# A written plan for the preparation of rows in a feed-forward stage, six relu buffers, and two folds moved ahead

## The chip, the cores and the metric

The kernel runs on one core of one Trainium2 chip. A core has five engines that run side by side, each through its own list of instructions in order: TensorE (PE in the profile, with PEld for its weight loads) multiplies matrices into PSUM, VectorE (DVE) and ScalarE (ACT) work elementwise and read PSUM and SBUF, GpSimd (POOL) works elementwise on SBUF, and SyncE (SP) issues transfers. An engine that reaches an instruction whose input isn't there stops, and everything behind it in its list stops too. The metric is the device time of one execution in microseconds (us), the median of several runs; a profiled execution gives a trace of every instruction.

## The reference

Only what is computed matters here:

```
def reference(A_x, A_w_r, A_w_i, B_x, B_w1, B_b1, B_w2, B_b2):
    x = A_x                                             # 1 x 2048 x 512, bf16
    X = rfft2(layernorm(x)) * (A_w_r + 1j * A_w_i)      # 2048 x 257 weights
    h = x + irfft2(X).bf16()
    r = relu(layernorm(h) @ B_w1 + B_b1)                # 512 -> 1792
    return h + (r * r) @ B_w2 + B_b2                    # 1792 -> 512
```

A spectral filter over both axes with a residual, then a feed-forward part with squared relu and another residual. Layer norms have no learned scale; each is over the 512 columns of a row.

## The kernel before

Everything is one core's work and stays in SBUF. The 2048 rows are kept as 16 groups of 128 rows. The Fourier transforms are matmuls against tables of sines and cosines that the kernel makes itself.

*First stage (lines 204 to 330).* For each group a row's mean and variance are found, by `bn_stats` and `bn_aggr` on VectorE (`ln1_stats`) or by two passes with accumulation on ScalarE (`ln1_sums`). `ln1_rstd` makes (variance + epsilon) to the power -0.5 with two GpSimd instructions. `ln1_fold` multiplies a table KF by it, one VectorE instruction for each group, into KFr, and `stage1` uses KFr as the moving operand of two groups' matmuls. The rows of x come in five loads: groups 0-1, 2-3, 4-7, 8-11, 12-15. Around the change the order is: statistics of groups 0 and 1, scale of 0 and 1, statistics of groups 2 and 4 (interleaved: both `bn_stats`, then both `bn_aggr`), folds of 0 and 1, `stage1(0)`.

*Middle (lines 340 to 530)*: three more transform stages and the product with the spectral weights in eight pairs of frequencies, ending in the tile T2 for all groups at once. The change doesn't touch it.

*Feed-forward part (lines 540 to 815).* The groups are taken in five chunks: CHUNKS = (0,1), (2-4), (5-8), (9-12), (13-15). A chunk of n groups is a moving operand of 128n columns. `mlp_slots(c)` makes its list of slots: 14 `up` slots, each four matmuls of W1 against UT into one PSUM bank `ph` (three of them), then a relu on ScalarE into a buffer `rl`, then the square on VectorE into `act`; then for each group three `down` slots of 5, 5 and 4 matmuls against W2 into a bank `po` (two of them), after which VectorE adds `hb` (that is h + b2, made on GpSimd, line 729, told to wait for the squares of f = 1, 4, 7, 10 of the chunk) and the result is stored. The last group of all is done in two halves (`last`).

While chunk c runs, chunk c + 1 is prepared. Its steps for a group g are:

- `s5`: four TensorE matmuls into a bank `pp` (three banks serve `pp`), the last transform along the columns, then two ScalarE copies out of it into V and H.
- `s5b`: four VectorE instructions that combine even and odd parts of V and H into R.
- `s6`: one TensorE matmul of R into a `pp` bank, the last transform along the rows.
- `s6a`: VectorE adds x and gives h (tile `hs`), which frees the bank.
- `s6b`: the statistics of h, on ScalarE for every second group of a chunk from 2 on (two passes, `on_act`), else on VectorE.

After all groups: `rstd` (square root on ScalarE, reciprocal on VectorE), `norm` (one VectorE instruction for each group, into u), and `transp` twice: TensorE transposes, one half of the columns each, with one ScalarE copy and one VectorE copy into UT, the operand of the next chunk's `up` slots.

What sets the order is a planner. `run(c)` walks through the slots, adds up their modelled TensorE costs (0.22 for each group of an `up` slot and so on), and after each slot puts out the preparation pieces that are due. `prep_steps` gives each piece a due time, by formula: evenly spaced rounds of s6(g-2), s5(g), s5b(g-1), s6a and s6b(g-2), from about 2n + 7.5 before the chunk's end to 7.3 before it, then `rstd`, `norm`, and the two `transp` at 2.4 and 1.7 before the end. `pin` then fixes this order on every engine, so the program's order is each engine's order.

Of the kernel before, what the change touches and what calls it, by code (L numbers as in the profile page):

```python
# [9 lines left out]
ALU = mybir.AluOpType  # L10
ACT = mybir.ActivationFunctionType
FP32 = mybir.dt.float32
BF16 = mybir.dt.bfloat16
I32 = mybir.dt.int32
I16 = mybir.dt.int16
P = 128
# [18 lines left out]
def kernel(  # L35
# [16 lines left out]
    nc = tc.nc  # L52
# [7 lines left out]
    EPS = 1e-5  # L60
# [41 lines left out]
    def after(ins, first, why):  # L102
        tc.add_manual_dep(ins.ins, first.ins.name,
                          mybir.DependencyInfo(mybir.DependencyClass.Sync, mybir.DependencyReason.DATA), reason=why)
        return ins
# [105 lines left out]
    def ln1_stats(*mine):  # L211
        sts = {}
        for k in range(len(mine) + 1):
            if k < len(mine):
                g = mine[k]
                sts[g] = st = fwd.tile([P, 6], FP32, tag="st", bufs=4, name="st")
                nc.vector.bn_stats(st[:], xs[:, g, :])  # L217
            if k > 0:
                g = mine[k - 1]
                nc.vector.bn_aggr(mv1[:, g, :], sts.pop(g)[:])  # L220

    def ln1_rstd(a, b):
        nc.gpsimd.tensor_scalar(rs1[:, a:b], mv1[:, a:b, 1], EPS, None, ALU.add)
        nc.gpsimd.tensor_tensor(rs1[:, a:b], rs1[:, a:b], mhalf[:, 0:b - a], ALU.pow)

    def ln1_fold(a, b, eng=nc.vector):
        for g in range(a, b):
            last = eng.tensor_scalar(KFr[:, g, :], KF[:], rs1[:, g:g + 1], None, ALU.mult)  # L228
        return last
# [32 lines left out]
    def angles_c(sl):  # L262
        return nc.gpsimd.tensor_scalar(fiE[1][:].rearrange("p (a b) -> p a b", a=9)[:, sl],
                                       fiE[0][:].rearrange("p (a b) -> p a b", a=9)[:, sl], 1.0, float(QT), ALU.mult,
                                       ALU.add)
# [8 lines left out]
    after(nc.gpsimd.tensor_scalar(fiG[:, 0:256], idxL[:, 0:256], cols[:, 0:1], float(QT), ALU.mult, ALU.add), fk,  # L274
          "the angles of the first stage first")
    nc.gpsimd.tensor_scalar(fiG[:, 256:512], idxL[:, 256:512], cols[:, 0:1], float(HT), ALU.mult, ALU.add)
    ln1_rstd(0, 2)
    ln1_stats(2, 4)
    f01 = ln1_fold(0, 2)
    after(angles_c(slice(0, 9)), f01, "not beside the folds")  # L280
    stage1(0, 12)
    ln1_sums(13)
# [273 lines left out]
    def s5(g, ahead=False):  # L556

        pe = bank("p5", "po", 2) if ahead else bank("p5", "pp", 3)  # L560
        for lt, tb, o in ((1, GI[:, 1, 0:129], 0), (3, GI[:, 3, 1:128], 129), (0, GI[:, 0, 0:128], 256),
                          (2, GIa[:, 1024:1152], 384)):
            nc.tensor.matmul(pe[:, o:o + tb.shape[1]], lhsT=T2[:, 2 * (lt % 2) + lt // 2, g].rearrange("p q s -> p (q s)"), rhs=tb,  # L563
                             start=True, stop=True)

        def rest():
            V = ffn.tile([P, 2, 2, 128], BF16, tag="V", bufs=3, name="V")
            H = ffn.tile([P, 2, 256], BF16, tag="H", bufs=3, name="H")
            nc.scalar.copy(V[:].rearrange("p e h c -> p (e h c)"), pe[:])  # L569
            nc.scalar.copy(H[:, :, 0:129:128], pe[:].rearrange("p (e h c) -> p e h c", e=2, h=2)[:, :, :, 0])  # L570
            Rs[g] = V, H

        if ahead:
            return rest
        rest()
# [38 lines left out]
    def s6(g):  # L614
        py = bank("p6", "pp", 3)
        if g == 0:
            nc.tensor.matmul(py[:], lhsT=identW[:], rhs=xs[:, 0, :], start=True, stop=False)
            nc.tensor.matmul(py[:], lhsT=KI[:], rhs=Rs.pop(g)[:], start=False, stop=True)
            nc.scalar.activation(hs[:, 0, :], py[:], ACT.Copy, scale=WSC, accum_out=mv2[:, 0, 0:1])
            return  # L620
        nc.tensor.matmul(py[:], lhsT=KI[:], rhs=Rs.pop(g)[:], start=True, stop=True)  # L621
        Ys[g] = py

    def s6a(g):
        nc.vector.scalar_tensor_tensor(hs[:, g, :], Ys.pop(g)[:], WSC, xs[:, g, :], ALU.mult, ALU.add)  # L625
# [16 lines left out]
    def on_act(c, g):  # L642

        return g == 0 if c < 2 else (g - CHUNKS[c][0]) % 2 == 0
# [23 lines left out]
    def transp(c, half):  # L668
# [13 lines left out]
        else:  # L682
            nc.vector.tensor_copy(dst, src)

    def prep_steps(c, total):

        a, b = CHUNKS[c]
        n = b - a
        first = 2 if c == 1 else 0
        end = total - 7.3  # L690
        t0 = 1.2 if c == 1 else total - 0.5 - 2.0 * n - 7.0
        gap = (end - t0) / (n + 1 - first)
        t0 = end - (n + 1) * gap
        steps = [(0.4, 0, rest[1])] if c == 1 else []
        for k in range(first, n + 2):
            t = t0 + k * gap
            if k >= 2:
                steps.append((t, 0.22, lambda g=a + k - 2: s6(g)))
            if k < n:
                steps.append((t, 0.22, lambda g=a + k: s5(g)))  # L700
            if 1 <= k <= n:
                steps.append((t + 0.1, 0, lambda g=a + k - 1: s5b(g)))
            if k >= 2:
                steps.append((t + 0.1, 0, lambda g=a + k - 2: (s6a(g), s6b(g, on_act(c, g)))))
        t = t0 + (n + 1) * gap
        steps.append((t + 1.6, 0, lambda: rstd(c)))
        steps.append((t + 2.2, 0, lambda: norm(c)))
        steps.append((total - 2.4, 0.12 * n, lambda: transp(c, 0)))
        steps.append((total - 1.7, 0.12 * n, lambda: transp(c, 1)))
        return steps  # L710

    def mlp_slots(c):
        a, b = CHUNKS[c]
        n = P * (b - a)
        UT = UTs[c]
        act = ffn.tile([P, NF, 512], BF16, tag="act", bufs=2, name="act")
        slots = []

        def up(f):
            ph = bank("ph", "ph", 3)  # L720
            for d in range(ND):
                nc.tensor.matmul(ph[:, 0:n], lhsT=W1[:, d, bass.ts(f, P)], rhs=UT[:, d, 0:n],  # L722
                                 start=(d == 0), stop=(d == ND - 1))
            rl = ffn.tile([P, 512], BF16, tag="rl", bufs=3, name="rl")
            nc.scalar.activation(rl[:, 0:n], ph[:, 0:n], ACT.Relu, bias=b1f[:, f:f + 1], scale=1.0)  # L725
            sq = nc.vector.tensor_tensor(act[:, f, 0:n], rl[:, 0:n], rl[:, 0:n], ALU.mult)  # L726
            mine = [a + f // 3] if c and f % 3 == 1 and f // 3 < b - a else range(a, b) if not c and f == NF - 1 else []
            for g in mine:
                add = nc.gpsimd.tensor_tensor(hb[:, g, :], hs[:, g, :], b2b[:], ALU.add)  # L729
                tc.add_manual_dep(add.ins, sq.ins.name,  # L730
                                  mybir.DependencyInfo(mybir.DependencyClass.Sync, mybir.DependencyReason.DATA),
                                  reason="not before this square")

        state = {}

        def last(i):
            g = a + i
            ot = ffn.tile([P, D], BF16, tag="ot", bufs=3, name="ot")
            for h in range(2):
                po = bank("po", "po", 2)  # L740
                sl = slice(256 * h, 256 * h + 256)
                for f in range(NF):
                    nc.tensor.matmul(po[:, 0:256], lhsT=act[:, f, bass.ts(i, P)], rhs=W2[:, f, sl], start=(f == 0),  # L743
                                     stop=(f == NF - 1))
                nc.vector.tensor_tensor(ot[:, sl], po[:, 0:256], hb[:, g, sl], ALU.add)
                nc.sync.dma_start(ov[:, g, sl], ot[:, sl])

        def down(i, f0, f1):
            if c == 4 and i == b - a - 1:
                return last(i) if f0 == 0 else None  # L750
            if f0 == 0:
                state[i] = bank("po", "po", 2)
            po = state[i]
            for f in range(f0, f1):
                nc.tensor.matmul(po[:], lhsT=act[:, f, bass.ts(i, P)], rhs=W2[:, f, :], start=(f == 0), stop=(f == NF - 1))  # L755
            if f1 == NF:
                g = a + i
                ot = ffn.tile([P, D], BF16, tag="ot", bufs=3, name="ot")
                nc.vector.tensor_tensor(ot[:], po[:], hb[:, g, :], ALU.add)  # L759
                nc.sync.dma_start(ov[:, g, :], ot[:])  # L760

        for f in range(NF):
            slots.append((0.22 * (b - a), lambda f=f: up(f)))
        for i in range(b - a):
            for f0, f1 in ((0, 5), (5, 10), (10, NF)):
                slots.append((0.22 * (f1 - f0), lambda i=i, f0=f0, f1=f1: down(i, f0, f1)))
        return slots
# [76 lines left out]
```

## Time and profile before

The time is 172.0 us, the median of three runs (171.52 to 172.26). The profiled execution's span is 171.0 us, at full TensorE clock.

| engine | busy us | share |
|---|---|---|
| TensorE | 154.7 | 90% |
| VectorE | 127.6 | 75% |
| ScalarE | 108.7 | 64% |
| GpSimd | 37.2 | 22% |

The first 20 us load and normalize; from 20 to 54 the transforms run; the first `up` matmul of chunk 0 starts at 54.39, those of chunks 1 to 4 at 70.50, 94.40, 122.40 and 149.38; the last matmul ends at 167.7 and the last store lands at the end of the span. A busy share says how long an engine had something in it, and is an average over stages with different limits. A wait, by contrast, names the engine that was waited for. In lists of waits the columns are the total us, the number of waits and the longest. In timelines they are start, length, engine, line, operation, output and input, and in brackets the idle time before it and what ended that. Runs of the same line are merged ("x6").

### The profile page before, as it was taken

How to read it: one execution, taken by the hardware profiler on the slowest of the kernel's cores; microseconds unless marked ns; L12 is line 12 of the kernel's file. 1: busy time of each engine (PE TensorE's matmuls, PEld its weight loads, DVE VectorE, ACT ScalarE, POOL GpSimd, SP SyncE). 2: the span in 40 equal slices, each digit the busy share in tenths (PEclk: the TensorE clock that was granted, in tenths of full speed). 3: DMA queues.
4: the chain of work that ended last, by engine and by line, in shares of the span. 5: the costliest groups of instructions: out<-in, count | busy, mean ns of one | idle time of the engine just before them, and what ended most of it. 6: DMA issues, size and time to landing. Idle time of an engine off the chain costs nothing.

```text
span 171.0 us, 2777 instructions
## 1 busy us (share of the span) xinstructions
PE 154.7 (90%) x976; PEld 89.0 (52%) x976; DVE 127.6 (75%) x319; ACT 108.7 (64%) x201; POOL 37.2 (22%) x65
## 2 busy tenths in 40 slices
PE   3679999899898889998699999999999999999992
PEld 1257667677754663565235444544544454456461
DVE  7799899999847888589597577698767587578320
ACT  4799887999956652498624677554377634478200
POOL 7588850000000005052000135000025200025000
PEclk9999999999999999999999999999999999999999
DMA  5997299996000000100000100000100000010011
GB/s 125 345 287 89 76 190 201 395 359 86 0 0 4 0 0 2 58 9 0 0 0 31 61 4 0 2 31 31 35 31 0 0 33 31 24 41 0 0 59 33
DMA packets 12622, 11.42 MB, mean 67 GB/s; under 512 B 6977, under 2 KB 11073, under 8 KB 12609
## 3 DMA queue, kind: packets, MB, share of 16 engines
q1 hardware_dynamic: 12448, 10.33, 21.8%
q0 software_dynamic: 160, 0.92, 2.5%
q8 instruction: 7, 0.11, 0.3%
q14 instruction: 7, 0.05, 0.1%
HBM read 8.01 MB, written 2.10 MB: 59 GB/s over the span
## 4 chain that ended last, share of the span: by engine, by line
PE 48%; DVE 35%; ACT 6%; issue 4%; DMA 3%; POOL 1%; SPq 0%; DVEq 0%; ACTq 0%
PE ph L722 23%; PE po L755 11%; DVE hs L625 5%; DMA xs<-in_A_x_dram 3%; DVE st L639 3%; DVE act L726 3%; DVE st L217 2%; ACT rl L725 2%; PE p L344 2%; PE p L677 2%; DVE ot L759 2%; DVE mA L434 2%; ACT junk L636 2%; PE po L743 2%; DVE mB L434 2%
## 5 line engine op out<-in xcount | busy, mean ns | idle before, releaser
L722 PE MATMUL ph<-UT,W 128*128 128x384 bf16 (+2 forms) x280 | 50.3, 336 | 1.8 <-ACT rl L725 1.1
L725 ACT ACTIVATE rl<-ph,b1f 128x384 bf16<-128x384 f32 (+2 forms) x70 | 41.3, 605 | 14.9 <-PE ph L722 10.3
L755 PE MATMUL po<-W,act 128*128 128x512 bf16 x210 | 49.1, 379 | 0.0
L726 DVE TENSOR_TENSOR act<-rl 128x384 bf16<-128x384 bf16 (+2 forms) x70 | 34.1, 514 | 16.2 <-ACT rl L725 15.9
L729 POOL TENSOR_TENSOR hb<-hs,b2b 128x512 f32<-128x512 bf16 x16 | 18.4, 1152 | 95.9 <-DVE act L726 95.9
L722 PEld LDWEIGHTS <-W 128*128 128x128 bf16 x280 | 27.1, 98 | 23.2 <-issue 2.4
L755 PEld LDWEIGHTS <-act 128*128 128x128 bf16 x210 | 20.0, 98 | 23.5 <-issue 2.4
L759 DVE TENSOR_TENSOR ot<-po,hb 128x512 bf16<-128x512 f32 x15 | 10.3, 688 | 7.4 <-PE po L755 5.6
L569 ACT CAST V<-p 128x512 bf16<-128x512 f32 x14 | 8.1, 581 | 5.5 <-PE p L563 5.5
L625 DVE SCALAR_TENSOR_TENSOR hs<-p,xs 128x512 bf16<-128x512 f32 x15 | 10.3, 684 | 0.9 <-PE p L621 0.9
L636 ACT ACTIVATE junk<-hs 128x512 bf16<-128x512 bf16 x6 | 3.8, 630 | 10.6 <-DVE hs L625 10.6
L243 PE MATMUL p<-KFr,xs 128*128 128x256 bf16 x32 | 7.3, 273 | 3.0 <-DVE KFr L228 2.9
L257 PE MATMUL p<-ones 128*128 128x512 bf16 x23 | 7.1, 453 | 2.8 <-POOL ones L153 2.8
L681 ACT COPY UT<-p 128x768 bf16<-128x768 bf16 (+1 forms) x4 | 3.6, 905 | 8.4 <-PE p L677 8.4
L217 DVE BATCH_NORM_STATS2 st<-xs 128x6 f32<-128x512 bf16 x12 | 7.9, 681 | 1.1 <-DMA xs<-in_A_x_dram 1.1
L621 PE MATMUL p<-R,KI 128*128 128x512 bf16 x15 | 5.7, 379 | 3.1 <-DVE R L612 3.1
L245 PE MATMUL p<-KFr,xs 128*128 128x256 bf16 x32 | 7.3, 272 | 0.0
L257 PEld LDWEIGHTS <-ones 128*128 128x128 bf16 x35 | 3.6, 108 | 6.7 <-POOL ones L153 2.8
L344 PE MATMUL p<-GF,Bt 128*128 128x256 bf16 x56 | 7.1, 273 | 0.0
L489 ACT CAST T<-p 128x1024 bf16<-128x1024 f32 x7 | 7.1, 1040 | 0.0
L639 DVE BATCH_NORM_STATS2 st<-hs 128x6 f32<-128x512 bf16 x9 | 6.3, 695 | 0.3
L374 ACT CAST U<-p 128x1024 bf16<-128x1024 f32 x6 | 6.2, 1058 | 0.0
(186 smaller groups left out, 230.9 us busy)
## 6 DMA issues: line engine op xcount, KB each, us to landing
W<-in_B_w_dram SPq DMA_DIRECT2D x2, 1792.0 KB, 10.0
out_dram<-ot SPq DMA_DIRECT2D x15, 128.0 KB, 1.8
xs<-in_A_x_dram SPq DMA_DIRECT2D x3, 512.0 KB, 6.6
WB<-in_A_w_r_dram SPq DMA_DIRECT2D x1, 578.2 KB, 6.0
WB<-in_A_w_i_dram SPq DMA_DIRECT2D x1, 578.2 KB, 7.2
xs<-in_A_x_dram SPq DMA_DIRECT2D x2, 256.0 KB, 3.9
b2b<-in_B_b_dram SPq DMA_DIRECT2D x1, 128.0 KB, 9.4
out_dram<-ot SPq DMA_DIRECT2D x2, 64.0 KB, 1.5
```

Source lines behind the costliest of these rows:

```text
L217: nc.vector.bn_stats(st[:], xs[:, g, :])
L257: nc.tensor.matmul(o, lhsT=ones[:, 0:P], rhs=ones[:], start=True, stop=True)
L344: nc.tensor.matmul(puv[:, :, e, :], lhsT=Bt[:, 2 * t + 1 - e, 2 * pr + q, :], rhs=GFv[:, t, :, e, :], start=(t == 0), stop=(t == 1))
L569: nc.scalar.copy(V[:].rearrange("p e h c -> p (e h c)"), pe[:])
L625: nc.vector.scalar_tensor_tensor(hs[:, g, :], Ys.pop(g)[:], WSC, xs[:, g, :], ALU.mult, ALU.add)
L639: nc.vector.bn_stats(st[:], hs[:, g, :])
L722: nc.tensor.matmul(ph[:, 0:n], lhsT=W1[:, d, bass.ts(f, P)], rhs=UT[:, d, 0:n], start=(d == 0), stop=(d == ND - 1))
L725: nc.scalar.activation(rl[:, 0:n], ph[:, 0:n], ACT.Relu, bias=b1f[:, f:f + 1], scale=1.0)
L726: sq = nc.vector.tensor_tensor(act[:, f, 0:n], rl[:, 0:n], rl[:, 0:n], ALU.mult)
L729: add = nc.gpsimd.tensor_tensor(hb[:, g, :], hs[:, g, :], b2b[:], ALU.add)
L755: nc.tensor.matmul(po[:], lhsT=act[:, f, bass.ts(i, P)], rhs=W2[:, f, :], start=(f == 0), stop=(f == NF - 1))
L759: nc.vector.tensor_tensor(ot[:], po[:], hb[:, g, :], ALU.add)
```

## The change

Three edits.

1. In the first stage the folds of groups 0 and 1 come after the statistics of group 2 and ahead of those of group 4. The addition of epsilon for these two groups goes from GpSimd to VectorE.
2. `prep_steps` no longer computes due times; it reads them from a table PLAN, one list for each of chunks 1 to 4. Every piece has its own entry, `s6a` and `s6b` too, which used to go together. Times for chunk 1 count from the start of chunk 0, the others from the end of the chunk before them (negative: that long before its end). The aim is to put each piece where the engines have room for it.
3. The relu tile `rl` has six buffers for three.

```diff
-    ln1_rstd(0, 2)
-    ln1_stats(2, 4)
+    nc.vector.tensor_scalar(rs1[:, 0:2], mv1[:, 0:2, 1], EPS, None, ALU.add)
+    nc.gpsimd.tensor_tensor(rs1[:, 0:2], rs1[:, 0:2], mhalf[:, 0:2], ALU.pow)
+    ln1_stats(2)
     f01 = ln1_fold(0, 2)
+    ln1_stats(4)
     after(angles_c(slice(0, 9)), f01, "not beside the folds")
...
+    PLAN = {
+        1: ((-3.33, 'ahead', 0),
+            (-0.19, 's5b', 1),
+            (1.74, 's5', 2),
+            (1.90, 's6', 0),
+            (2.59, 's5b', 2),
+            (3.15, 's6', 1),
+            (4.46, 's6a', 0),
+            (5.01, 's6b', 0),
+            (5.71, 's6a', 1),
+            (5.93, 's6', 2),
+            (6.26, 's6b', 1),
+            (8.49, 's6a', 2),
+            (9.04, 's6b', 2),
+            (9.66, 'rstd', 0),
+            (11.25, 'norm', 0),
+            (15.74, 't0', 0),
+            (17.95, 't1', 0),),
+        2: ((-20.48, 's5', 0),
+            (-19.75, 's5b', 0),
+            (-19.10, 's5', 1),
+            (-18.37, 's5b', 1),
...
+            (-2.74, 't0', 0),
+            (-1.51, 't1', 0),),
...
     def prep_steps(c, total):
...
-        first = 2 if c == 1 else 0
-        end = total - 7.3
-        t0 = 1.2 if c == 1 else total - 0.5 - 2.0 * n - 7.0
-        gap = (end - t0) / (n + 1 - first)
...
-                steps.append((t + 0.1, 0, lambda g=a + k - 2: (s6a(g), s6b(g, on_act(c, g)))))
...
+        return [(t if c == 1 else total + t, pieces[p][0], lambda p=p, k=k: pieces[p][1](a + k)) for t, p, k in PLAN[c]]
...
-            rl = ffn.tile([P, 512], BF16, tag="rl", bufs=3, name="rl")
+            rl = ffn.tile([P, 512], BF16, tag="rl", bufs=6, name="rl")
```

The table is best seen in what it does to TensorE's order. In the two programs it is as follows (UP3: three `up` slots; DN5: five down matmuls; S5 and S6: of one group; TR: transposes of one group, all four column blocks; the numbers of instructions are the same in both). First before, then changed, a line for each chunk that runs:

```
before
0: UP3 S6 S5 UP6 S6 UP5 DN5 S6 DN19 TR3 DN4
1: UP9 S5 UP2 S5 UP2 S6 S5 UP1 DN5 S6 S5 DN5 S6 DN9 S6 DN19 TR4 DN4
2: UP14 S5 DN5 S5 DN9 S6 S5 DN5 S6 S5 DN5 S6 DN9 S6 DN19 TR4 DN4
3: UP14 DN5 S5 DN5 S5 DN9 S6 S5 DN5 S6 DN4 S6 DN24 TR3 DN4
changed
0: UP4 S5 S6 UP3 S6 UP5 S6 UP2 DN28 TR3
1: UP2 S5 UP1 S5 UP2 S5 UP2 S5 S6 UP1 S6 UP2 S6 UP2 S6 UP2 DN38 TR4 DN4
2: UP4 S5 UP2 S5 UP2 S5 UP2 S5 UP2 S6 UP2 DN5 S6 DN5 S6 DN9 S6 DN33 TR4 DN4
3: UP1 S5 UP1 S5 UP1 S5 UP7 S6 UP1 S6 UP1 S6 UP2 DN38 TR1.5 DN9 TR1.5 DN9
```

VectorE's order in chunk 1 goes from 11 squares, s5b, 2 squares, s5b, s6a, square, s5b, s6a, statistics, and so on, to 2 squares, s5b, 2 squares, s5b, 2 squares, s5b, square, s6a, s5b, 2 squares, s6a, 2 squares, s6a, square, s6a, 2 squares, statistics, output add, statistics, reciprocal, norm. In chunk 0 it goes to square, s5b, 4 squares, s5b, 4 squares, s6a, square, statistics, 2 squares, s6a, square, statistics, square, s6a, statistics, output add, reciprocal, norm.

More of the change, by code (lines that the diff above doesn't have):

```diff
@@ L683, in transp @@
             nc.vector.tensor_copy(dst, src)
+    PLAN = {
[20 more added lines that the diff above has]
+            (-18.37, 's5b', 1),
+            (-17.72, 's5', 2),
+            (-16.99, 's5b', 2),
+            (-16.34, 's5', 3),
+            (-16.27, 's6', 0),
+            (-15.71, 's6a', 0),
+            (-15.61, 's5b', 3),
+            (-14.89, 's6', 1),
+            (-14.33, 's6a', 1),
+            (-13.51, 's6', 2),
+            (-12.95, 's6a', 2),
+            (-12.13, 's6', 3),
+            (-11.94, 's6b', 0),
+            (-11.57, 's6a', 3),
+            (-10.56, 's6b', 1),
+            (-9.18, 's6b', 2),
+            (-7.80, 's6b', 3),
+            (-6.57, 'rstd', 0),
+            (-6.30, 'norm', 0),
+            (-2.74, 't0', 0),
+            (-1.51, 't1', 0),),
+        3: ((-24.63, 's5', 0),
+            (-22.53, 's5', 1),
+            (-22.25, 's5b', 0),
+            (-20.43, 's5', 2),
+            (-20.15, 's5b', 1),
+            (-18.33, 's5', 3),
+            (-18.05, 's5b', 2),
+            (-15.99, 's6', 0),
+            (-15.95, 's5b', 3),
+            (-14.29, 's6a', 0),
+            (-13.89, 's6', 1),
+            (-13.10, 's6b', 0),
+            (-12.19, 's6a', 1),
+            (-11.79, 's6', 2),
+            (-11.00, 's6b', 1),
+            (-10.09, 's6a', 2),
+            (-9.69, 's6', 3),
+            (-8.90, 's6b', 2),
+            (-7.99, 's6a', 3),
+            (-6.80, 's6b', 3),
+            (-6.16, 'rstd', 0),
+            (-5.30, 'norm', 0),
+            (-2.35, 't0', 0),
+            (-1.48, 't1', 0),),
+        4: ((-25.83, 's5', 0),
+            (-24.89, 's5', 1),
+            (-23.95, 's5', 2),
+            (-23.67, 's5b', 0),
+            (-22.73, 's5b', 1),
+            (-21.79, 's5b', 2),
+            (-17.57, 's6', 0),
+            (-16.63, 's6', 1),
+            (-15.69, 's6', 2),
+            (-12.12, 's6a', 0),
+            (-11.18, 's6a', 1),
+            (-10.24, 's6a', 2),
+            (-9.86, 's6b', 0),
+            (-8.92, 's6b', 1),
+            (-7.98, 's6b', 2),
+            (-6.58, 'rstd', 0),
+            (-6.48, 'norm', 0),
+            (-4.96, 't0', 0),
+            (-2.74, 't1', 0),),
+    }
@@ L688, in prep_steps @@
         n = b - a
-        first = 2 if c == 1 else 0
-        end = total - 7.3
-        t0 = 1.2 if c == 1 else total - 0.5 - 2.0 * n - 7.0
-        gap = (end - t0) / (n + 1 - first)
[L693 to L703, printed above, removed]
-                steps.append((t + 0.1, 0, lambda g=a + k - 2: (s6a(g), s6b(g, on_act(c, g)))))
[L705 to L710, printed above, removed]
+        pieces = dict(s5=(0.22, s5), s5b=(0, s5b), s6=(0.22, s6), s6a=(0, s6a), s6b=(0, lambda g: s6b(g, on_act(c, g))),
+                      ahead=(0, lambda g: rest[1]()), rstd=(0, lambda g: rstd(c)), norm=(0, lambda g: norm(c)),
+                      t0=(0.12 * n, lambda g: transp(c, 0)), t1=(0.12 * n, lambda g: transp(c, 1)))
+        return [(t if c == 1 else total + t, pieces[p][0], lambda p=p, k=k: pieces[p][1](a + k)) for t, p, k in PLAN[c]]
     def mlp_slots(c):
```

## The prediction

> **What bounds the kernel now.** I read the page first (PE 90% of the span, DVE 75%, ACT 64%), then the busy time in five stretches, one for each chunk of the feed-forward part, cut where the first up-projection matmul of a chunk starts.
>
> ```profile
> 54.39:70.50 16.11, 14.54 (x104) 9.40 (x105) 12.78 (x41) 7.84 (x20) 2.26 (x2) 1.00 0.03 10
> 70.50:94.40 23.90, 21.46 (x136) 11.61 (x135) 18.88 (x47) 14.63 (x33) 3.45 (x3) 1.00 0.04 15
> 94.40:122.40 28.00, 27.31 (x149) 13.08 (x148) 20.84 (x49) 16.72 (x33) 4.60 (x4) 1.00 0.06 20
> 122.40:149.38 26.98, 26.74 (x141) 12.54 (x140) 18.18 (x41) 15.97 (x31) 4.61 (x4) 1.00 0.06 18
> 149.38:168.20 18.82, 18.36 (x113) 10.86 (x111) 9.89 (x19) 8.13 (x14) 3.46 (x3) 1.00 0.09 31
> ```
>
> Columns: stretch, length, then busy us and count of PE, PEld, DVE, ACT, POOL, clock, DMA. TensorE is the engine to keep fed: its clock is full throughout, and the last chunk, which prepares nothing, is matmul after matmul. Busy time hides short holes, so I count a floor from the chain's issue rates: 56 up matmuls of 512 columns in 12.09 us (0.216 each), 56 of 384 in 9.10 (0.1625), 256 columns 0.109 by the spacing of the first stage, 19 down matmuls in 4.10 (0.216), s5 or s6 of a group 0.22, 16 transposes in 1.04 (0.065). Chunk 0: 6.10 up + 6.05 down + 0.22 (one s5) + 0.65 (three s6) + 0.78 (12 transposes) = 13.80, took 16.11: lost 2.3. Chunk 1: 9.10 + 9.07 + 0.87 + 0.87 + 1.04 = 20.95 of 23.90: lost 2.95. Chunk 2: 12.09 + 12.10 + 2.78 = 26.97 of 28.00: lost 1.0. Chunk 3: 24.19 + 2.08 = 26.27 of 26.98: lost 0.7. So 7.0 us is to be had in the stretch that the plan rewrites.
>
> The list of waits says who causes it (total us, times, longest):
>
> ```profile
> DVE act L726 <- ACT rl L725: 15.9, 38, 2.1
> ...
> ACT rl L725 <- DVE act L726: 3.2, 2, 1.8
> ...
> PE p L621 <- DVE R L612: 3.1, 5, 1.7
> ...
> PE ph L722 <- ACT rl L725: 1.1, 2, 1.0
> ```
>
> TensorE's own holes are s6 (L621) waiting for the combined rows R, and up-projections waiting for relu. The timelines place them. First ScalarE in chunk 0, then TensorE, and VectorE in chunk 1:
>
> ```profile
> 59.92 2.51 ACT L725 ACTIVATE rl<-ph,b1f 128x256 bf16<-128x256 f32 x6 [1.44 <-DVE act L726]
> 64.20 0.84 ACT L725 ACTIVATE rl<-ph,b1f 128x256 bf16<-128x256 f32 x2 [1.77 <-DVE act L726]
> ```
>
> ```profile
> 85.56 0.38 PE L621 MATMUL p<-R,KI 128*128 128x512 bf16 x1 [1.66 <-DVE R L612]
> ```
>
> ```profile
> 84.21 0.36 DVE L726 TENSOR_TENSOR act<-rl 128x384 bf16<-128x384 bf16 x1 [2.10 <-ACT rl L725]
> 84.48 0.28 DVE L607 TENSOR_TENSOR H<-V 128x254 bf16<-128x254 bf16 x1
> ```
>
> In chunk 0 s5b, s6a and s6b of a group (57.08 to 59.56) stand before three squares; with three relu buffers ScalarE stops and TensorE 0.95 us later. In chunk 1 the formula puts s6a, statistics on ScalarE, one relu, one square and the next s5b in a row, so each s6 waits for the whole ring of engines.
>
> In the first stage the chain goes through a load and then two folds:
>
> ```profile
> 7.42 0.69 DVE L217 BATCH_NORM_STATS2 st<-xs 128x6 f32<-128x512 bf16 x1 [0.94 <-DMA xs<-in_A_x_dram]
> 8.03 0.30 DVE L220 BATCH_NORM_AGGREGATE mv<-st 128x2 f32<-128x6 f32 x2
> 8.25 0.47 DVE L228 TENSOR_SCALAR KFr<-KF,rs 128x256 bf16<-128x256 bf16 x2
> ```
>
> Their scale was ready at 6.94 (the power on GpSimd runs from 6.21 for 0.73), but the queue held them behind the statistics of group 4, whose rows came at 7.42.
>
> **What the Trainium skill says.** "TensorE: Matmul & The Clock Gate", section "Wait — 56ns, not 53.3ns?", gives a warm spacing of N/2.4 ns plus about 2.5: 216 ns at 512 columns and 162.5 at 384. The trace agrees (0.216, 0.1625). "SBUF — State Buffer", section "Who interferes with whom", says that a VectorE operation with two SBUF inputs and a GpSimd operation that reads SBUF exclude one another for a whole instruction. The trace agrees: a square that takes 0.42 alone started at 97.91 beside the bias add of 97.55 to 98.70 and took 1.07. "Perfetto Trace Analysis", section "Optimization Strategy", reads a recurring bubble as possibly too few buffers; the two ScalarE waits above are that.
>
> **The change part by part.**
>
> *Folds ahead.* The sum with epsilon goes from GpSimd (0.23) to VectorE (0.17), adds one handover, and drops one. Sums ready at 5.58, add to 5.75, power behind GpSimd's angle table (ends 5.80) to about 6.6, statistics of group 2 to 6.5 with aggregate to 6.6, folds about 6.7 to 7.2: all inside the 0.94 us wait for the rows of group 4. So the 0.47 of folds leave the queue that is solid from 7.42 to 14.5. ScalarE is nearly solid as well (5.8 to 19.6; idle only 0.25 at 15.05 and 0.16 at 18.99, and 0.07 before 12.88): it gives 0.4. Bounds 0.3 to 0.47; I take 0.4. The next scale on GpSimd does not block: the angles of the next table wait for the folds and end at about 8.7 rather than 9.97, before the sums of group 5.
>
> *Chunk 0 (prepares groups 2 to 4).* The order is now 4 ups, s5, s6, 3 ups, s6, 5 ups, s6, 2 ups, all 28 downs, then all 12 transposes. VectorE: from s5b of group 3 at 56.1, two s5b (0.94 each), 13 squares at 0.20, three s6a (0.71), three statistics (0.83): 9.1 us plus small waits for relu, so to about 65.4, where it ended at 66.8. The last square is done at about 64.0 instead of 65.2. Six buffers let relu run ahead: 14 relus at 0.42 and two evictions of 0.52 from 55.09 end at 62.0. TensorE's ups end at 54.39 + 6.10 + 0.87 = 61.4 without a hole; downs 61.4 to 67.45 (the last down of the first group, at 64.2, just meets its square). Output add to 66.1, reciprocal, and normalization, held by the second bias add on GpSimd to 66.4, ends at 67.4. Here the plan gives something back: no downs stand behind the transposes, so the copy of the first half (0.80 on ScalarE) is bare: transposes to 67.84, copy to 68.8, next chunk at 68.9. It took 16.1 us, now 14.5: gain 1.6. Best case 1.65 (the bare copy stays), worst 0.7 if VectorE slips by 0.9.
>
> *Chunk 1 (groups 5 to 8).* s5 go in from the third up, s5b between squares. Starting at 68.9, VectorE has 14 squares at 0.29, four s5b at 0.94, four s6a at 0.62: 10.3 us in an up-projection of 9.1 + 1.74 = 10.8. What the trace of before doesn't show is s5b beside the bias adds: they are started by the squares of f = 1, 4, 7, and in front of the plan's s5b. Bounds: nothing, or 3 times 1.15 if each holds VectorE for its length. I take about 1 each, as the square at 97.91 lost 0.65 having come 0.36 late. Then R of group 7 comes at about 77.4 for an s6 due at 76.75 (0.65 lost), and R of group 8 at 79.3, due with that delay at 79.1 (0.2 to 0.4 more): 1.1 lost, where 2.95 was: gain 1.85. Later squares are met by downs that take 3 us per group, and normalization is done about a microsecond before the transposes. Range of this gain 0.3 to 2.8.
>
> *Chunk 2 (9 to 12) and 3 (13 to 15).* All s5b are done among the ups, the s6 come late and find R ready. VectorE in chunk 2: 14 squares at 0.36 + 3.76 + up to 4.6 of bias adds = 13.4 against 13.2 us of ups; squares end at about 14.6 and the last down of group one needs its square at about 16. Normalization ends some 1.1 us before the transposes: 0.1 lost, gain 0.9. In chunk 3 normalization ends at about 21.4 for transposes at 21.6: 0.2 lost, gain 0.5. Two slots of downs, 9 matmuls each, hide the copies there.
>
> *Buffers* cost nothing: SBUF space only. They're what lets s5b stand before squares; their own worth is counted in chunk 0.
>
> Sum: 0.4 + 1.6 + 1.85 + 0.9 + 0.5 = 5.25 us. 172.0 - 5.25 = 166.75; I say 166.7.
>
> **The rivals.**
> 1. *The plan fills nearly all* (6.6 us: 7.0 less the bare copy 0.67, plus 0.4, rounded down): 165.4. For it: only VectorE's order and three buffers make the holes. Against: the bias adds.
> 2. *A new wait takes over in chunks 0 and 1*: normalization ends after the bare transposes are due, and s5b behind GpSimd's lock holds s6. Chunk 1 then keeps nothing and chunk 0 half: 0.4 + 0.8 + 0 + 0.9 + 0.5 = 2.6, 169.4. For it: in both, VectorE's sum is within 0.5 us of TensorE's.
> 3. *Slower*: bias adds and s5b delay squares in chunks 1 to 3 until relu buffers and the PSUM banks run out; 11 adds at 1.15 less 0.3 that is hidden each = 9.4, 172.0 - 5.25 + 9.4 = 176. For it: VectorE has 13.4 us of work in 13.2. Against: six buffers hold up to 5 us of ups, and downs start with early squares.
>
> **How the numbers follow.** Forecast 0.62, rival 1 0.15, rival 2 0.16, rival 3 0.05, no change 0.02. The range 165.0 to 169.2 takes in the first rival and most of the second. Faster by over 0.5% (under 171.1) 0.93, same 0.02, slower 0.05.
>
> **What would show it.** Right: folds of groups 0 and 1 before 7.4 us; no ScalarE wait on squares; TensorE's s6 waits 3.1 down to about 1, all in chunk 1; transposes after chunk 0 followed by a hole of some 0.7 us; chunk lengths 14.5, 22.0, 27.1, 26.5. Wrong: waits of transposes for normalization over 0.5 us, up matmuls waiting for relu, s5b operations over 1 us in every chunk with TensorE idle after them.

## The result and the profile after

The changed kernel takes 166.57 us (166.57 to 166.60), the kernel before 172.02 in the same series: ratio 0.9687 (0.9666 to 0.9709), 5.45 us less where 5.3 was forecast. The profiled span goes from 171.0 to 164.8, which is 6.2; the difference of 0.75 turns out to be the profile of before, not the change (below).

The stretches of the first four chunks, cut as before at the first up-projection of each:

```profile
53.65:68.13 14.48, 13.93 (x104) 9.42 (x105) 12.69 (x42) 7.95 (x20) 2.26 (x2) 1.00 0.03 11
68.13:90.14 22.01, 21.15 (x135) 11.61 (x134) 17.44 (x47) 13.91 (x33) 3.55 (x3) 1.00 0.06 19
90.14:116.97 26.83, 26.83 (x150) 13.12 (x149) 20.83 (x49) 16.10 (x33) 4.91 (x4) 1.00 0.06 21
116.97:143.13 26.16, 26.16 (x141) 12.61 (x139) 18.22 (x41) 15.31 (x31) 4.72 (x4) 1.00 0.06 21
```

Chunk 0 went from 16.11 to 14.48, chunk 1 from 23.90 to 22.01, chunk 2 from 28.00 to 26.83, chunk 3 from 26.98 to 26.16: 5.5 us in all. In chunks 2 and 3 TensorE's busy time (the number behind the comma) equals the stretch: not one hole is left. The waits of TensorE from 53 to 143 us are three (`UT` is the operand of the up-projection, `rl` a relu buffer):

```profile
PE p L623 <- ACT rl L797: 0.8, 1, 0.8
PE ph L794 <- DVE UT L881: 0.6, 1, 0.6
PE ph L794 <- ACT UT L683: 0.6, 1, 0.6
```

The second is the start of chunk 0, there before too. The third is the bare copy after chunk 0, the first the one s6 of chunk 1 that still waits. ScalarE's wait for squares (3.2 us before) is gone from the list. In time on TensorE:

```profile
66.74 0.83 PE L679 MATMUL p<-ident,u 128*128 128x128 bf16 x12
68.13 1.46 PE L794 MATMUL ph<-UT,W 128*128 128x384 bf16 x8 [0.55 <-ACT UT L683]
...
74.67 1.46 PE L794 MATMUL ph<-UT,W 128*128 128x384 bf16 x8
76.89 0.38 PE L623 MATMUL p<-R,KI 128*128 128x512 bf16 x1 [0.76 <-ACT rl L797]
```

and on VectorE and then GpSimd at the same place:

```profile
74.77 1.24 DVE L609 TENSOR_TENSOR H<-V 128x254 bf16<-128x254 bf16 x1
75.93 0.28 DVE L610 TENSOR_TENSOR H<-V 128x254 bf16<-128x254 bf16 x1
76.25 0.29 DVE L613 TENSOR_TENSOR R<-H 128x256 bf16<-128x256 bf16 x1
76.46 0.28 DVE L614 TENSOR_TENSOR R<-H 128x256 bf16<-128x256 bf16 x1
```

```profile
74.66 1.20 POOL L801 TENSOR_TENSOR hb<-hs,b2b 128x512 f32<-128x512 bf16 x1 [2.77 <-DVE act L798]
```

The first instruction of s5b of group 7 takes 1.24 us in place of 0.28, as long as GpSimd's bias add stands beside it. R is complete at 76.74, and s6 starts 0.15 later. The trace names a relu as releaser; the time of R says otherwise, and two experiments (e5 and e9 below) settle it.

In the first stage the folds now stand ahead of group 4:

```profile
6.69 0.48 DVE L228 TENSOR_SCALAR KFr<-KF,rs 128x256 bf16<-128x256 bf16 x2
7.09 0.69 DVE L217 BATCH_NORM_STATS2 st<-xs 128x6 f32<-128x512 bf16 x1
```

There is no wait for rows at 7.09 at all, where before VectorE waited 0.94 us until 7.42.

### The profile page after: what moved, and what is told of

It reads as the page before. It is cut to its first block, busy times and chain, and to the rows that moved or that the text cites. A ratio compares the mean times of both kernels' runs of the same rounds, so it can differ in the third digit from the quotient of the medians.

```text
span 164.8 us, 2760 instructions
## 1 busy us (share of the span) xinstructions
PE 153.8 (93%) x976; PEld 89.5 (54%) x976; DVE 126.3 (77%) x320; ACT 106.7 (65%) x201; POOL 37.9 (23%) x64
## 4 chain that ended last, share of the span: by engine, by line
PE 68%; DVE 16%; ACT 5%; DMA 3%; POOL 2%; issue 2%; SPq 0%; ACTq 0%; DVEq 0%
PE po L827 28%; PE ph L794 25%; DMA xs<-in_A_x_dram 3%; PE p L346 2%; DVE mA L436 2%; PE po L815 2%; DVE mB L436 2%; ACT junk L209 2%; PE p L623 2%; PE p L679 2%; DVE Z L442 1%; POOL rs L224 1%; ACT rl L797 1%; DVE Z L443 1%; PE p L565 1%
## 5 line engine op out<-in xcount | busy, mean ns | idle before, releaser
L794 PE MATMUL ph<-UT,W 128*128 128x384 bf16 (+2 forms) x280 | 52.7, 336 | 1.2 <-DVE UT L881 0.6
L827 PE MATMUL po<-W,act 128*128 128x512 bf16 x210 | 47.3, 379 | 0.0
L801 POOL TENSOR_TENSOR hb<-hs,b2b 128x512 f32<-128x512 bf16 x16 | 18.9, 1184 | 89.2 <-DVE act L798 89.2
L798 DVE TENSOR_TENSOR act<-rl 128x384 bf16<-128x384 bf16 (+2 forms) x70 | 29.8, 458 | 10.1 <-ACT rl L797 10.0
L257 PE MATMUL p<-ones 128*128 128x512 bf16 x23 | 8.2, 511 | 2.8 <-POOL ones L153 2.8
L609 DVE TENSOR_TENSOR H<-V 128x254 bf16<-128x254 bf16 x14 | 6.9, 490 | 0.3 <-ACT V L571 0.2
L655 ACT ACTIVATE sd<-mv,eps 128x2 f32<-128x2 f32 (+2 forms) x7 | 2.0, 295 | 6.7 <-DVE mv L642 6.6
```

Of the source, the lines that this page charges most:

```text
L257: nc.tensor.matmul(o, lhsT=ones[:, 0:P], rhs=ones[:], start=True, stop=True)
```

## The experiments

My theory: the plan removes holes that VectorE's order made; folds, buffers and plan add up; what is left is GpSimd's lock in chunk 1 and the bare copy in chunk 0. Rivals: the buffers do most of it; the folds are worth the 0.74 us by which the traces differ at the start of chunk 0; or nothing. Every run below was timed beside the kernel before, whose median was 172.01 to 172.11.

**One part at a time.**

```diff
 e1_folds: before, with edit 1 alone
 e2_buffers: before, with
-            rl = ffn.tile([P, 512], BF16, tag="rl", bufs=3, name="rl")
+            rl = ffn.tile([P, 512], BF16, tag="rl", bufs=6, name="rl")
 e3_plan_3buf: before, with edit 2 alone
 e4_plan_6buf: before, with edits 2 and 3
```

Expected of the folds: 

> The kernel before with the folds of groups 0 and 1 moved ahead alone. Theory (the folds leave a VectorE queue that is solid, ScalarE is nearly solid too): 0.4 us faster, 171.6, first up-projection matmul about 54.0 in the profile. Rival (the fold moved the first stage by 0.74, as the two traces differ): 171.3. Rival (the difference of the traces is the arrival of the rows of x, which changes from run to run): no more than 0.1, 171.9.

Expected of the buffers: 

> The kernel before with six relu buffers alone. Theory (the buffers serve the plan; with the formula VectorE's order is what holds TensorE): ScalarE's two waits on squares, 3.2 us, are gone, but TensorE gets back only the 0.95 us hole of chunk 0 at most, since squares and normalization come as late as before: 171.5, chunk 0 15.6 to 16.1 us. Rival (the buffers are the change): chunk 0 14.5 and 170.4 or less.

Expected of the plan with three buffers: 

> The written plan alone, with three relu buffers and the folds where they were. Theory (the plan puts two s5b and bias adds ahead of squares, which three buffers don't bridge): relu waits for squares in chunks 0 and 1, 0.3 and 1 us lost on TensorE, 168.3, and more waits of relu on squares than before. Rival (the plan alone carries it): 167.0, as with six.

Expected of the plan with six: 

> The written plan with six buffers, folds where they were. Theory (edits add up, folds are worth 0.4): 167.0, chunk lengths 14.5, 22.0, 26.8, 26.2 as in the changed kernel. Rival (folds worth 0.74): 167.3. Rival (a start earlier by 0.4 is absorbed later): 166.6.

| kernel | us (lowest to highest) | ratio to before | chunks 0, 1, 2, 3 |
|---|---|---|---|
| before | 172.11 (171.77 to 172.99) | 1 | 16.11, 23.90, 28.00, 26.98 |
| e1_folds | 172.24 (172.22 to 173.78) | 1.0008 (0.9996 to 1.002) | 16.11, 23.89, 28.01, 27.14 |
| e2_buffers | 170.90 (170.71 to 171.41) | 0.9931 (0.9909 to 0.9952) | 15.04, 23.90, 28.01, 26.96 |
| e3_plan_3buf | 167.09 (166.88 to 167.22) | 0.9702 (0.968 to 0.9723) | 14.77, 22.10, 26.82, 26.17 |
| e4_plan_6buf | 166.79 (166.24 to 167.34) | 0.9689 (0.9662 to 0.9717) | 14.48, 22.02, 26.83, 26.16 |

The plan alone gives 5.0 of the 5.45 us. It moves work in the queues of TensorE, ScalarE and VectorE at once; how much of the 5.0 belongs to which queue was not tried. My expectation for it with three buffers, 168.3, was too gloomy: chunks 0 and 1 lose 0.3 and 0.1, not 0.3 and 1. ScalarE does wait for squares (2.7 us in chunks 0 and 1), but TensorE loses only a small part of that. I take the slack to be the three `ph` banks; no run shows it. ScalarE's waits for squares in e3:

```profile
ACT rl L795 <- DVE act L796: 2.7, 3, 1.3
```

The buffers alone give 1.2 us, 1.07 of it in chunk 0 (the other chunks keep their lengths), which is midway between my expectation and its rival: with the waits of 1.44 and 1.77 gone, the last statistics of chunk 0 start 10.54 us after its first matmul (63.91 - 53.37) and no longer 11.60 (65.99 - 54.39); the copies and transposes follow. So I was wrong that squares and normalization come as late with six buffers. In chunks 1 to 3 the lengths are those of before, so three buffers were not what held TensorE there. The parts don't add up: 1.2 alone, 0.3 on top of the plan.

The folds alone give nothing (172.24 against 172.11). That is the term of my sum that fell.

**Why the folds give nothing.** In each trace I set the start of group 4's statistics against the first up-projection matmul:

| kernel | statistics of group 4 | first up | difference |
|---|---|---|---|
| before | 7.42, waits for rows | 54.39 | 46.97 |
| e2_buffers | 6.40, waits | 53.37 | 46.97 |
| e3_plan_3buf | 6.71, waits | 53.67 | 46.96 |
| e4_plan_6buf | 6.57, waits | 53.54 | 46.97 |
| changed | 7.09, no wait | 53.65 | 46.56 |
| e1_folds | 7.08, no wait | 53.64 | 46.56 |

The 0.41 us that I worked out is there, from that start on. But the same load lands anywhere between 6.40 and 7.42 in these runs, and the folds can't come before the power on GpSimd ends (6.66), so they hold group 4's statistics until 7.09. Rows at 7.42 gain 7.42 + 46.97 - (7.42 + 46.56) = 0.41; rows at 6.40 lose 7.09 + 46.56 - (6.40 + 46.97) = 0.28; break-even is 6.68. The median of before agrees: it is 0.70 us under the profiled run of before (172.81), which had its rows at 7.42, so its rows come at about 6.7 (an estimate from these times), where the edit gains about 0.05 us. Against that chunk 3 of e1 is 0.16 us longer than before's; -0.11 is left, and -0.13 was measured.

To test the rule, I made rows come surely late (the second number of `stage1` is how many matmuls on ones go ahead of it, to keep TensorE busy):

```diff
-    CH = ((0, 2), (2, 4), (4, 8), (8, 12), (12, 16))
+    CH = ((0, 2), (2, 4), (8, 12), (4, 8), (12, 16))
-    for g in (3, 7, 11):
+    for g in (3, 11, 7):
 e7_late_load: before with this; e8_late_load_folds: also edit 1
 e10_late_folds_warm: e8, and
-    stage1(2, 6)
+    stage1(2, 18)
```

Expected of the late load: 

> The kernel before with the loads of groups 4 to 7 and 8 to 11 in the other order, and ScalarE's sums of groups 7 and 11 too, so that the rows of group 4 come later. Read against its twin with the folds moved. Theory (first up-projection = start of the statistics of group 4 + 46.97): it starts some 0.5 to 1.5 us later and the kernel takes 172.6 to 173.6.

Expected of the late load with folds: 

> The same late load with the folds moved ahead. Theory (the fold edit pays only where VectorE waits for rows at that point): 0.4 us less than its twin, the first up-projection at the start of the statistics of group 4 + 46.56. Rival (the edit is worth nothing whenever the rows come, because ScalarE's queue is solid): the same as its twin within 0.15 us.

e7 took 174.56 us (174.15 to 174.88), e8 174.76 (173.93 to 175.49). For e7 I had expected 172.6 to 173.6, counted from the median of before; its profiled run, 174.22, is 1.41 above the profiled run of before. The first up-projection of e7 is at 8.86 + 46.97 = 55.83, as it should. That of e8 is at 56.70 = 8.89 + 47.81, worse. The times speak for the rival, but the trace doesn't: its folds of groups 2 to 5 start at 12.56 against 12.93. Then TensorE, idle for 3.37 us since the early `stage1(0)`, runs at half clock (stretch, length, busy us of PE, PEld, DVE, ACT, POOL, clock, DMA; kernel e8, with the first matmul after the idle time ahead):

```profile
12.87 0.27 PE L243 MATMUL p<-KFr,xs 128*128 128x256 bf16 x1 [3.37 <-DVE KFr L228]
...
12.00:14.00 2.00, 1.13 (x7) 0.88 (x7) 2.00 (x9) 0.97 (x4) 1.24 (x3) 0.80 1.76 279
14.00:16.00 2.00, 2.00 (x12) 1.40 (x10) 2.00 (x9) 1.01 (x1) 1.72 (x4) 0.50 0.57 130
16.00:18.00 2.00, 2.00 (x15) 1.41 (x14) 1.83 (x6) 1.22 (x2) 1.63 (x5) 0.85 0.08 16
```

So that experiment measured a second thing. The runs of e8 show its size: the three with a mean clock of 0.989 to 0.990 took 175.25 to 175.49 us, the three with 0.999 to 1.000 took 173.93 to 174.26, which is under e7. The clock was low in e7 too, in all five runs (means of 0.987 to 0.990), after an idle time of 2.69 us, though earlier, in `stage1(0)`: 0.50 from 10 to 12 us, and still below 1 in the next stretch:

```profile
10.01 0.37 PE L243 MATMUL p<-KFr,xs 128*128 128x256 bf16 x1 [2.69 <-DVE KFr L228]
...
12.00:14.00 2.00, 2.00 (x9) 0.90 (x8) 2.00 (x10) 1.97 (x4) 1.57 (x3) 0.71 1.48 253
```

There it cost nothing that reaches the feed-forward part: the distance is still 46.97. e10 is e8 with its idle time filled with matmuls on ones:

Expected: 

> e8_late_load_folds with 12 more warming matmuls ahead of the second pair of groups, so that TensorE isn't idle for 3.4 us there. Theory (the late twin with folds lost 1.3 us to a halved TensorE clock after the idle time, and the folds themselves give 0.4): full clock from 12 to 20 us, first up-projection at the start of the statistics of group 4 + 46.56, some 0.4 under e7_late_load, 174.1. Rival (the folds give nothing when rows are late, or the clock isn't the cause): still 174.6 or more.

It took 173.87 us (173.51 to 175.48), with full clock:

```profile
12.00:14.00 2.00, 1.40 (x14) 1.22 (x13) 2.00 (x9) 1.04 (x3) 1.34 (x2) 1.00 1.39 278
14.00:16.00 2.00, 2.00 (x18) 1.60 (x17) 1.97 (x9) 1.75 (x3) 1.72 (x4) 1.00 0.51 112
```

Statistics of group 4 at 8.66, first up at 55.22: 46.56. The theory holds in the traces. The medians of e7 and e10 (174.56, 173.87) go the same way, but with rows that land at different times they don't measure 0.4 by themselves.

**What is left in chunks 0 and 1.**

```diff
 e5_no_lock: changed kernel, with a fill for the add (leaves out h + b2)
-                add = nc.gpsimd.tensor_tensor(hb[:, g, :], hs[:, g, :], b2b[:], ALU.add)
+                add = nc.gpsimd.memset(hb[:, g, :], 0.0)
 e6_cover: changed kernel, and
-        return g == 0 if c < 2 else (g - CHUNKS[c][0]) % 2 == 0
+        return g in (0, 3) if c < 2 else (g - CHUNKS[c][0]) % 2 == 0
-            (6.26, 's6b', 1),
+            (7.10, 's6b', 1),
-            (15.74, 't0', 0),
-            (17.95, 't1', 0),),
+            (12.00, 't0', 0),
+            (12.10, 't1', 0),),
 e9_cover_and_adds: e6, and
-            mine = [a + f // 3] if c and f % 3 == 1 and f // 3 < b - a else ...
+            mine = {1: [2], 13: [3, 4]}.get(f, []) if c == 1 else [a + f // 3] if ...
```

Expected of no lock: 

> The changed kernel with the 16 bias adds replaced by fills with zero that read nothing (h and b2 are left out of the sum that is stored). Theory (GpSimd's reads hold the first instruction of s5b for about 1 us twice in chunk 1, and that makes the one hole before s6): no s5b instruction over 0.5 us, the hole of 0.76 us gone, chunk 1 21.1 to 21.2 instead of 22.0, 165.7. Rival (the hole is ScalarE's, which the trace names as releaser): hole stays, 166.5.

Expected of the covered copies: 

> The changed kernel with the statistics of group 3 on ScalarE, after the relus, and the transposes of chunk 1 ahead of the last four down matmuls of chunk 0. Theory (VectorE's statistics set when normalization ends, and the hole of chunk 0 is the bare copy behind the transposes): normalization ends 0.8 us earlier, the copies lie behind 0.86 us of downs, chunk 0 13.9 instead of 14.5, 166.0. Rival (ScalarE's two passes, 1.6 us, come later than VectorE's statistics would have): normalization no earlier, transposes wait, 166.6 or more.

Expected of both mended: 

> The changed kernel with statistics of group 3 on ScalarE and the transposes of chunk 1 ahead of the last four downs (as in e6_cover), and in chunk 1 the second and third bias add told to wait for the square of f = 13 instead of 4 and 7. Theory (the second add holds s5b of group 7; late adds stand beside statistics and output adds[...]): the hole before s6 is gone, chunk 1 20.8 to 21.0, 164.7, without leaving anything out. Rival (the adds now hold the late squares or normalization, and the downs wait): 165.3 or more.

e5 took 165.37 us (165.34 to 165.45): chunk 1 20.82, 1.19 less, and no wait of TensorE in it. The same instruction as above, in e5, with GpSimd's fill (0.52 us from 74.04) beside it:

```profile
74.19 0.28 DVE L609 TENSOR_TENSOR H<-V 128x254 bf16<-128x254 bf16 x1
```

e6 took 165.79 us (165.76 to 166.12), 0.78 less than the changed kernel: normalization ends at 65.85 (66.56 in the changed kernel), chunk 0 takes 13.76, and downs stand where the hole was, behind the transposes:

```profile
65.87 0.83 PE L679 MATMUL p<-ident,u 128*128 128x128 bf16 x12
66.54 1.03 PE L827 MATMUL po<-W,act 128*128 128x512 bf16 x4
67.40 1.46 PE L794 MATMUL ph<-UT,W 128*128 128x384 bf16 x8
```

e9 took 164.83 us (164.82 to 164.91), ratio 0.9580 (0.9568 to 0.9592), with chunks 13.76, 21.00, 26.83 and 26.16 and no wait of TensorE in the list after the first up-projection. It leaves nothing out and beats the changed kernel by 1.74 us. Chunk 1 is 0.18 us longer than in e5: its first add still holds s5b of group 5 (1.26 us), and R of group 8 comes that much late. The late adds stand beside statistics and output adds, which take 0.69 us as they do without an add:

```profile
80.63 2.27 POOL L801 TENSOR_TENSOR hb<-hs,b2b 128x512 f32<-128x512 bf16 x2 [9.53 <-DVE act L798]
...
80.47 0.69 DVE L641 BATCH_NORM_STATS2 st<-hs 128x6 f32<-128x512 bf16 x1
81.74 0.69 DVE L831 TENSOR_TENSOR ot<-po,hb 128x512 bf16<-128x512 f32 x1 [0.36 <-PE po L827]
```

The rivals of these three runs fall: the hole in chunk 1 isn't ScalarE's, statistics on ScalarE don't come too late, and the late adds don't hold anything that matters.

## Why the prediction was right, and where not

*Folds, 0.4.* This step failed: "all inside the 0.94 us wait for the rows of group 4" took one trace's wait for a property of the kernel. The wait is 0.24, 0.42, 0.55 and 0.94 in four traces with unchanged loads and folds. Measured gain: none alone, 0.2 beside the plan (166.79 against 166.57, within the spread of the first). What the edit does do is to make the time steady, since rows that land before 7.09 no longer set it: 21 of 22 runs of e1 lie between 172.22 and 172.26 (the other took 173.78), those of before between 171.77 and 172.99. The rows also explain the difference of 0.75 in the section on the result: the profiled run of before had late rows and took 172.81 us, 0.8 above its median.

*Chunk 0, 1.6.* Measured 1.63. The reasons hold: ups and downs without a hole, normalization ready 12.9 us after the first up-projection (66.56 - 53.65, where I had 67.4 - 54.39 = 13.0), transposes behind the downs at 66.74, a bare copy, 0.55 of idle time. In e6 the copy is covered and normalization comes earlier, and chunk 0 is 0.72 shorter, without a wait; the two edits of e6 were not tried apart.

*Chunk 1, 1.85.* Measured 1.89. The trace shows idle times of 0.76 before s6 of group 7 and 0.1 before that of group 8. By the starts of the matmuls it is more: eight ups from 74.67 at 0.1625 make s6 of group 7 due at 75.97, and it starts at 76.89, 0.92 late (I had 0.65); that of group 8 is due at 78.40 and starts at 78.67, 0.27 late (I had 0.2 to 0.4). Together that is 1.19, just what e5 gets back. The two first instructions of s5b that meet an add lose 0.96 to 0.98 each, I took about 1. e5 and e9 show the cause.

*Chunks 2 and 3, 0.9 and 0.5.* Measured 1.17 and 0.82. Mis-sized on two terms: I let transposes cost 0.065 us, from a row in which they waited for normalization, and they cost 0.056 (16 from 88.38 to 89.28); and I allowed 0.1 and 0.2 for losses that didn't come.

*Buffers.* Right that they cost nothing; wrong, in my expectation of e2, that alone they would give some half a microsecond.

So 5.25 came out near 5.45 partly by luck: one term was too large by 0.2 to 0.4 and two were too small by 0.6 together. Rival 1 (165.4) named what the kernel does once the adds are out of the way: e5 gave 165.37, partly by chance, since the rival counts 0.4 for the folds. Rival 2 took the waits for larger than they are: in chunk 0 normalization (66.56) ends before the transposes (66.74), and both adds of that chunk follow its last square and so every s5b (63.38; the f = 1, 4, 7, 10 of the description hold for the later chunks); in chunk 1 the adds cost 1.19 us, where 2.95 were lost before. For rival 3 TensorE would have to wait in chunks 2 and 3, and it does not, though adds stand beside instructions of s5b there as well (one of 1.24 us at 103.14, one of 1.26 at 124.48).

## What to carry to other kernels

Count the floor of the bounding engine from issue rates, stage by stage, then take each hole's cause from the completion time of its operand rather than from the name that the trace gives. Before crediting an edit that fills a wait for a load, see in several runs how long that wait is, or whether the distance from it to a later mark is constant. When an engine's queue is planned, plan as well the small work of another engine that can hold it, as GpSimd's adds did here.

## What the runs showed of the hardware

A load issued at the same place landed from 6.40 to 7.42 us after the start in four runs (before, e2, e3, e4). A VectorE instruction with two inputs in SBUF went from 0.28 to 1.24 us beside a GpSimd add of 1.20 us (changed kernel), and took 0.28 beside a fill that reads nothing (e5).

After 3.37 us without a matmul (e8) and after 2.69 us (e7) TensorE's granted clock was 0.50. It stayed there for about 3.4 us in e8 (estimated from the three stretches shown, with the clock either 1.00 or 0.50). The Trainium skill, "TensorE: Matmul & The Clock Gate", section "What's actually happening", gives half speed after at least one idle window of about 3.4 us. The half speed agrees; the 2.69 us of e7 are less than that window, so in this case a shorter gap was enough.

And e1, e8 and e10, the kernels with the formula and moved folds, have a chunk 3 of 27.14 us where the others with the formula have 26.96 to 26.98. In the traces of e1, e8 and e10 one VectorE instruction of s5b of group 14 starts 0.75 us after the one before it, in those of before and e7 0.39; why is open.
